# Four interleaved attention layers on one core: a new written order for stages and visits, layer 2's queries projected beside its keys, exps of projections from an SBUF copy

## The chip, the cores and the metric

The kernel runs on 1 core of a Trainium2 chip. The metric is the device time of one execution in microseconds; before the change it is 2619.29 us, the median of 3 runs (2614.57 to 2623.58). Line numbers (L1292) are those of the kernel before.

## The reference

x has 2048 tokens of 1024 features. Four layers follow one another: A, B, A, B, numbered 0 to 3 in the code. Each is `x = x + layer(layernorm(x))`, with 32 heads of 32 features; the two A layers share their weights, and so do the two B layers.

```python
# A: linear attention
pq = einsum("bhsd,hdf->bhsf", q, w_phi);  pk = einsum("bhsd,hdf->bhsf", k, w_phi)
phi_q = concat([softmax(pq), softmax(-pq)], -1);  phi_k = concat([softmax(pk), softmax(-pk)], -1)
kv = einsum("bhsf,bhsd->bhfd", phi_k, v);  z = einsum("bhsf->bhf", phi_k)
o = einsum("bhqf,bhfd->bhqd", phi_q, kv) / (einsum("bhqf,bhf->bhq", phi_q, z)[..., None] + 1e-6)
return o @ wo
# B: full softmax attention, no mask
p = softmax(einsum("bhqd,bhkd->bhqk", q, k) * 32**-0.5);  o = einsum("bhqk,bhkd->bhqd", p, v)
return o @ wo
```

In an A layer, kv and z need the keys and values of all 2048 tokens before the first output. In a B layer every query needs every key, but sums over keys can be collected in parts.

## The kernel before, in words

The 2048 tokens are 16 tiles of 128 (t or tg) and 4 chunks of 512 (c). The 1024 features are 8 groups of 128 (g, four heads each). A projection is a *task*: eight matmuls that sum over the features into one PSUM bank of 128 x 512 (`mm8`), and a `post` that empties the bank.

**The stages.** `AK` projects keys (with w_phi folded into the weights by `fold`) and values of an A layer, takes two exps of each key bank (of x and of -x, L737, on ACT), normalises them and sums kv and z in `kvacc`. `PQ` projects its queries for one chunk, with two exps of each bank (L841). `DN` forms the denominators and the outputs, `AO` the output projection, residual and layernorm. `BP` projects keys (into K2a, K2b), queries (to DRAM as qd) and values (V) of a B layer for one chunk and one half of the features. `BO` is its output projection. `PQ` needs the same transposed, normalised input (xnT) as `AK` of its chunk, so `spill` writes that input to DRAM (xs, 1 MB a chunk, POOL's queue) and `xslot` loads it again. xnT has two slots, and a third in kvacc while kvacc is not in use; they are granted in the order of the list `users`.

**Attention of a B layer** runs in *units*: a query range of 4 or 2 tiles, a pair of heads and some chunks of keys. A visit in the tuple `VISITS` is (first tile, tiles, chunks of keys, adds a stored part, finishes, half of the groups), and it stands for 8 units. Part sums that aren't finished go to DRAM (pd) and come back. A step of a unit is a few matmuls for scores into two double-bank tiles of PSUM (ring, three of them; L1312), an exp of 128 x 1024 on ACT for each (L1292, tile E), and matmuls of E with V and with ones into the bank acc (L1348). There are 2048 such exps, 1024 in each B layer; the model calls them exp_chain.

**Who sets the order.** Every engine's instruction order is written out when the kernel is built. A small clock in the kernel (`Clock`) imitates the engines with costs (MM, SEM, c_ps, c_act and others) and decides what is issued next. An attention step goes first whenever its unit is ready and two ring tiles are free; otherwise `pick` looks through the next 60 undone tasks, in the order in which the stages were built, and takes the first whose inputs, weight slab, buffers and bank are there. Within a unit list the visits are strictly in order. While attention is active (`att_active`), a background task has the single bank bg and its matmuls are split in four column strips (L402); when it isn't, free ring tiles serve as more banks, and matmuls are whole (L405). Then too, evictions (`cp`, L381 and L383) may go to ACT as well as DVE. While attention is active, the two exps of a key or query bank first wait 0.5 us of the clock's time (ACT_SLACK), and release the bank after the second.

Weights are slabs of 1 MB. Four slots hold them always; the stores of V and K2 serve as more when no attention uses them. POOL's queue loads them. SP's queue issues the other transfers and the DMA transposes of normalised inputs and A outputs. For chunks in the set `TR`, PE transposes those instead (`pe_tr`, L462), with an eviction. SBUF temporaries are 28 blocks of 128 x 1024 (`blk`); tokens such as t_phi, t_eq (8 each) limit how many blocks one kind may hold.

Of the kernel before, what the change touches and what calls it, by code (L numbers as in the profile page):

```python
# [18 lines left out]
P = 128  # L19
# [10 lines left out]
MM = 0.216  # L30
SWITCH = 0.105
SEM = 0.1
# [78 lines left out]
class Clock:  # L111
# [50 lines left out]
    def _op(self, gen, eng, cost, fn, lat=SEM):  # L162
        if isinstance(eng, tuple):
            eng = min(eng, key=lambda e: max(self.busy.get(e, 0.0), self.now))
# [51 lines left out]
class Task:  # L216
# [17 lines left out]
VISITS = (  # L234
# [29 lines left out]
def kernel(  # L264
# [72 lines left out]
    t_q, t_acc, t_part, t_R, t_tmp, t_ot = tok(2), tok(5), tok(6), tok(2), tok(3), tok(8)  # L337
# [11 lines left out]
    xsp = {(l, c): dd(f"xs{l}_{c}", [P, PO, C]) for l in (0, 2) for c in range(NC)}  # L349
# [58 lines left out]
    users = [(0, "K", c) for c in range(NC)]  # L408
    for l in (0, 2):
        if l == 2:  # L410
            users += [(2, "K", 0), (2, "K", 1), (2, "K", 2), (2, "Q", 0), (2, "K", 3)]
        else:
            users += [(0, "Q", 0)]
        users += [(l, "Q", 1), (l + 1, "B", 0), (l + 1, "B", 1), (l, "Q", 2), (l + 1, "B", 2),
                  (l, "Q", 3), (l + 1, "B", 3)]
# [29 lines left out]
    def ln_tail(u, t, xb, st):  # L445
# [6 lines left out]
        yield ("op", "V", c_sb(1024, 4), lambda e: nc.vector.tensor_scalar(  # L452
# [119 lines left out]
    def slab_plan():  # L572
        want = sorted((slab_next(s), s) for s in slab_use)
        for nxt, s in want[:12]:
# [8 lines left out]
            for i, sl in enumerate(slots):  # L583
                if not sl.avail or sl.users or sl.loading:
                    continue
                if i >= 4 and min((x for x in sl.limits if x > lo[0]), default=1 << 30) < nxt:
                    continue
# [119 lines left out]


    phi_b = {}
# [7 lines left out]
    def build_AK(l, c, prs=(0, 1), hs=(0, 1)):  # L717
        u = (l, "K", c)
        if u in TR and 0 in hs:
            for pr in prs:  # L720
# [3 lines left out]
        if 0 in prs and 0 in hs:  # L724
            clk.start(xslot(u, 17))
            clk.start(spill(u))

        def pk(t, h):
            tg = 4 * c + t

            def post(bank, rel, b):
                use_xn(u)
                e = b
                if att_active():
                    yield ("sleep", ACT_SLACK)
                for s in range(2):
                    yield ("op", "S", c_act(C), lambda x, s=s: nc.scalar.activation(  # L737
                        out=e[:, s * C:(s + 1) * C], in_=bank[:], func=ACT.Exp, scale=1.0 - 2.0 * s))
                rel()
# [5 lines left out]
                yield tt(("V", "P") if att_active() else "V", {"V": c_sb(1024), "P": c_pool(1024)}, e3, e3, rb, ALU.mult)  # L745
# [18 lines left out]
        def kv(pr, h, gi):  # L764
            tgs = [4 * c + 2 * pr, 4 * c + 2 * pr + 1]
# [3 lines left out]
            def mms():  # L769
                o = []  # L770
                for j, idx in enumerate(GRP[gi]):
                    gl, s = divmod(idx, 2)
                    for a, tg in enumerate(tgs):
                        def fn(bank, ct, W, j=j, gl=gl, s=s, a=a, tg=tg):
# [5 lines left out]
                                start=(j == 0 and a == 0), stop=(a == 1), skip_group_check=True)  # L780
# [3 lines left out]
            def post(bank, rel, b):  # L784
# [8 lines left out]
                if c == 0 and pr == 0:  # L793
# [4 lines left out]
                kv_n[l] = kv_n.get(l, 0) + 1  # L798
                if c == NC - 1 and pr == 1:
# [12 lines left out]
            add(f"kv{l}.{c}.{pr}.{h}.{gi}", needs, None, mms(), post)  # L812

        for h in hs:
# [4 lines left out]
            for pr in prs:  # L819
                for gi in range(3):  # L820
                    kv(pr, h, gi)
# [6 lines left out]
    n_cnt = {}  # L828

    def build_PQ(l, c):  # L830
# [3 lines left out]
        def pq(g):  # L834
            def post(bank, rel, b):
                use_xn(u)
                e = b
                if att_active():
                    yield ("sleep", ACT_SLACK)
                for s in range(2):  # L840
                    yield ("op", "S", c_act(C), lambda x, s=s: nc.scalar.activation(  # L841
                        out=e[:, s * C:(s + 1) * C], in_=bank[:], func=ACT.Exp, scale=1.0 - 2.0 * s))
                rel()
# [130 lines left out]
    def build_BP(l, c, h):  # L974
        u = (l, "B", c)
        if h == 0:
            clk.start(xslot(u, 24))
# [5 lines left out]
        def kk(g):  # L983
            gl = g % 4

            def post(bank, rel, b):
                use_xn(u)
                b4 = bank[:].rearrange("p (m e n) -> p m e n", m=2, e=2)
                yield cp(K2[0][c][h][:, gl], b4[:, :, 0, :], 256)
# [6 lines left out]
                None, ks_no[h, c // 2])  # L996

        def qq(g):
            gl = g % 4

            def post(bank, rel, b):
# [4 lines left out]
                for x in (0, 64):  # L1006
                    yield ("op", "V", c_sb(C, 4), lambda e, x=x: nc.vector.tensor_copy(
# [7 lines left out]
        def vv(t, h):  # L1015
            def post(bank, rel, b):
                use_xn(u)
                yield cp(Vc[c][h][:, t, :], bank[:], C)
                rel()
                clk.set(("V", l, c, t, h))  # L1020
            add(f"bv{l}.{c}.{t}.{h}", [("xt", u, t)], ("bv", h),
                mm8(lambda k, W: xn[u][:, k, t * P:(t + 1) * P], lambda k, W: W(k)), post,
                None, vs_no[h, c // 2])

        kk(4 * h)
        qq(4 * h)
        for t in range(4):
            vv(t, h)
# [470 lines left out]
```

## Time and profile before

| what | before |
|---|---|
| median of 3 runs | 2619.29 us |
| profiled execution, its own time | 2628.97 us |
| its span, first to last instruction | 2626.8 us |
| TensorE (PE) busy | 2304.8 us, 88% |
| ScalarE (ACT) busy | 2105.4 us, 80% |
| VectorE (DVE) busy | 1262.1 us, 48% |
| GpSimd (POOL) busy | 426.3 us, 16% |
| attention exps on ACT (L1292) | 2048, 1908.5 us |
| mean granted TensorE clock | 0.906 of full |
| first and last attention exp | 301.4 and 2612.8 us |

All times inside the execution are microseconds from the span's start. Busy time counts instructions in progress, each stretch once; overlapping exps have a mean of 1109 ns but pass every 0.93 us at best. A row of a group of instructions gives line, engine, operation, output<-inputs, shape and count, then busy time and mean ns of one, then idle time of the engine just before them and what ended it. A row of a stretch gives its bounds and length, busy times with counts, then the granted clock and DMA figures.

### The profile page before, as it was taken

What the parts mean: (1) busy time and instruction counts of PE and PEld (TensorE: products, weight loads), DVE (VectorE), ACT (ScalarE), POOL (GpSimd) and SP (SyncE); (2) the same over time, 40 slices, a digit from 0 to 9 for tenths busy, and PEclk for the clock granted to TensorE, in tenths of its full rate; (3) what the DMA queues carried; (4) which work ended last, traced back from release to release, by engine and by line L of the source; (5) the groups of instructions that cost most, each with busy time, mean ns of one, the idle gap of its engine ahead of it and who ended that gap; (6) DMA issues with size and microseconds to landing.
All of it is one profiled execution on the core that took longest, in us unless ns stands there. A gap on an engine that the chain in (4) does not pass through costs nothing. (4 is left out here: it accounts for less than half of the span.)

```text
span 2626.8 us, 65988 instructions
## 1 busy us (share of the span) xinstructions
PE 2304.8 (88%) x28190; PEld 925.2 (35%) x28250; DVE 1262.1 (48%) x2246; ACT 2105.4 (80%) x2443; POOL 426.3 (16%) x519
## 2 busy tenths in 40 slices
PE   6887898898999998998888889889899989899887
PEld 3444432333333222343444443233333322223333
DVE  5874741432344555874447575143244354464222
ACT  3533379597999999999993337959798999999998
POOL 3131200100110222331122220010021021122010
PEclk9998999899999989999999899989989998778777
DMA  7382562464353333342023345246334322231000
GB/s 241 109 212 85 163 203 97 131 164 141 78 147 116 122 98 124 90 140 55 26 80 113 117 134 169 93 127 180 111 106 147 113 90 77 81 100 49 18 20 21
DMA packets 198998, 294.79 MB, mean 112 GB/s; under 512 B 89904, under 2 KB 100144, under 8 KB 195632
## 3 DMA queue, kind: packets, MB, share of 16 engines
q1 hardware_dynamic: 171072, 176.28, 23.2%
q0 software_dynamic: 27632, 114.31, 13.2%
q8 instruction: 220, 3.60, 0.6%
q14 instruction: 74, 0.61, 0.1%
HBM read 191.95 MB, written 79.69 MB: 103 GB/s over the span
## 5 line engine op out<-in xcount | busy, mean ns | idle before, releaser
L1292 ACT ACTIVATE E<-ring 128x1024 bf16<-128x1024 f32 x2048 | 1908.5, 1109 | 152.8 <-PE ring L1312 150.7
L1348 PE MATMUL acc<-E,V 128*32 128x512 bf16 (+1 forms) x5120 | 710.7, 380 | 4.0 <-DVE blk L388 2.2
L1348 PE MATMUL acc<-E,ones 128*32 128x512 bf16 (+1 forms) x5120 | 710.4, 380 | 0.0
L1312 PE MATMUL ring<-Q,K2b 32*128 32x512 bf16 (+1 forms) x2560 | 438.7, 369 | 161.8 <-ACT E L1292 154.3
L1312 PE MATMUL ring<-Q,K2a 32*128 32x512 bf16 (+1 forms) x2560 | 459.6, 370 | 10.9 <-ACT E L1292 10.1
L1348 PEld LDWEIGHTS <-V 128*32 128x32 bf16 x5120 | 206.3, 101 | 309.9 <-issue 278.8
L1087 DVE COPY blk<-acc 128x512 f32<-128x512 f32 (+1 forms) x160 | 93.3, 583 | 428.3 <-PE acc L1348 419.9
L388 POOL TENSOR_TENSOR blk<-blk,blk 64x512 bf16<-64x512 f32 (+1 forms) x156 | 168.7, 1081 | 714.1 <-DVE blk L1121 643.2
L1312 PEld LDWEIGHTS <-K2a 32*128 32x128 bf16 x2560 | 123.6, 93 | 427.9 <-issue 420.7
L1312 PEld LDWEIGHTS <-K2b 32*128 32x128 bf16 x2560 | 155.0, 93 | 289.7 <-issue 284.3
L1121 DVE RECIPROCAL blk<-blk 128x128 f32<-128x128 f32 x252 | 223.0, 923 | 2.3
L388 DVE TENSOR_TENSOR blk<-blk,acc 128x512 f32<-128x512 f32 x128 | 87.3, 682 | 275.3 <-PE acc L1348 274.6
L1348 PEld LDWEIGHTS <-ones 128*32 128x32 bf16 x5120 | 201.6, 101 | 2.4 <-issue 0.4
L402 PE MATMUL bg<-slab,blk 128*32 128x512 bf16 x2532 | 170.8, 386 | 3.2 <-DVE blk L388 2.0
L402 PE MATMUL bg<-slab,xnT 128*32 128x512 bf16 x2076 | 152.2, 414 | 11.0 <-ACT blk L737 9.1
L402 PE MATMUL bg<-xnT,slab 128*32 128x512 bf16 x1596 | 113.0, 399 | 9.6 <-ACT blk L841 4.8
L405 PE MATMUL ring<-slab,xnT 128*128 128x512 bf16 x426 | 105.0, 386 | 12.9 <-DMA xnT<-blk 3.2
L388 DVE TENSOR_TENSOR blk<-blk,bg 128x512 bf16<-128x512 bf16 x106 | 72.1, 680 | 85.0 <-PE bg L402 76.7
L388 POOL TENSOR_TENSOR blk<-blk 128x256 bf16<-128x256 f32 x102 | 73.5, 730 | 227.3 <-DVE blk L388 226.3
L405 PEld LDWEIGHTS <-xnT 128*128 128x128 bf16 x729 | 71.4, 100 | 101.2 <-issue 18.4
L402 PEld LDWEIGHTS <-blk 128*32 128x32 bf16 x2896 | 78.2, 98 | 73.7 <-issue 16.2
L742 DVE TENSOR_REDUCE sm<-blk 128x32 f32<-128x1024 bf16 x64 | 77.5, 1212 | 50.3 <-ACT blk L737 50.1
(187 smaller groups left out, 2337.5 us busy)
## 6 DMA issues: line engine op xcount, KB each, us to landing
pd<-blk SPq DMA_DIRECT2D x128, 256.0 KB, 2.3
blk<-pd SPq DMA_DIRECT2D x128, 256.0 KB, 3.1
slab<-in_B_wqkv_dram POOLq DMA_DIRECT2D x28, 1024.0 KB, 7.3
Q<-qd SPq DMA_DIRECT2D x112, 256.0 KB, 2.7
qd<-blk SPq DMA_DIRECT2D x64, 256.0 KB, 2.2
x<-blk SPq DMA_DIRECT2D x48, 256.0 KB, 2.2
blk<-x SPq DMA_DIRECT2D x48, 256.0 KB, 4.0
slab<-in_A_wo_dram POOLq DMA_DIRECT2D x10, 1024.0 KB, 6.2
```

What stands on the lines that cost most here:

```text
L388: return ("op", e, cost, lambda x: eng(x).tensor_tensor(out=o, in0=a, in1=b, op=op))
L402: nc.tensor.matmul(o[js], lhsT=l[:, js], rhs=r, start=st, stop=sp, tile_position=(0, 32 * j), skip_group_check=True)
L405: nc.tensor.matmul(o, lhsT=l, rhs=r, start=st, stop=sp, skip_group_check=True)
L742: yield ("op", "V", c_sb(1024), lambda x: nc.vector.reduce_sum(out=sm[:, 0:32], in_=e3, axis=AX.X))
L1087: yield ("op", "V", c_ps(n), lambda e: nc.vector.tensor_copy(out=a, in_=acc_t[:, 0:n]))
L1121: yield ("op", "V", 0.1 + 0.0065 * P, lambda e, x=x: nc.vector.reciprocal(out=r[:, x:x + P], in_=r[:, x:x + P]))
L1292: yield ("op", "S", c_act(2 * n), lambda x: nc.scalar.activation(out=E[:, :, 0:n], in_=ring_t[buf][:, :, 0:n], func=ACT.Exp, scale=INV_SQR ...
L1312: nc.tensor.matmul(ring_t[bufs[e]][:, j, i * n:(i + 1) * n], lhsT=K2[e][c][u.g // 4][r, u.g % 4, m, :], rhs=u.Q[r, e, 0:n], start=True, st ...
L1348: nc.tensor.matmul(u.acc[r0 + 32 * j:r0 + 32 * j + 32, 0:n], lhsT=lh, rhs=E[:, j, i * n:(i + 1) * n], start=first, stop=final, tile_positi ...
```

## The change

It replaces the written-out list of stages by a table `STAGES` and the visits by two tables, `VIS1` and `VIS3`, one for each B layer. A visit now names single groups (0 to 7, four heads each) instead of a half; layer 1 has 24 visits (64 group loads of queries, 128 units), layer 3 has 29 (80 and 160); before, each had 18 (72 and 144). `BP` is cut into quarters of the features, and a unit waits for its quarter of V alone.

Layer 2's queries: `PQ(2, c)` goes. `PS(2, c)` projects them from the xnT of `AK(2, c)`, stores each bank as bf16 in DRAM (pqd, 128 KB, SP's queue), and `pq_loader` brings them back once layer 2's last keys have their input, for the two exps from SBUF. The spill and reload of layer 2's xnT goes.

`two_exps`: while attention is active, DVE copies a key or query bank to an SBUF block and releases the bank; both exps read the block. Otherwise they read the bank as before.

Beside that: kv sums of four tiles at once where a stage has both pairs (`KVM`; 81 tasks for 96 over a pair of layers as the table cuts them); normalising of phi_k may go to POOL also without attention; first weight loads spaced by 8 us; other chunks transposed by PE (`TR`); 26 blocks for 28; costs of the clock changed, among them MM2, SEM, PE_LAT and a choice of engine by end of work.

```diff
-VISITS = (
-    (0, 4, (0,), False, False, 0), (0, 4, (0,), False, False, 1),
-    (4, 4, (0, 1), False, False, 0), (0, 4, (1,), True, False, 0),
...
+VIS1 = (
+    (0, 4, (0,), False, False, (0, 1)), (0, 4, (1,), True, False, (0, 1)), (0, 4, (0, 1), False, False, (2, 3)),
+    (4, 4, (0, 1), False, False, (0, 1, 2, 3, 4, 5, 6, 7)), (0, 4, (0, 1), False, False, (6, 7)),
+    (0, 4, (0, 1), False, False, (4, 5)), (8, 4, (0, 1, 2), False, False, (4, 5)),
+    (8, 4, (0, 1, 2), False, False, (6, 7)), (0, 4, (2, 3), True, True, (0, 1, 2)),
...
+    (14, 2, (0, 1, 2, 3), False, True, (0, 3, 6, 7)), (14, 2, (0, 1, 2, 3), False, True, (4, 5)),
+    (14, 2, (0, 1, 2, 3), False, True, (1, 2)),
+VIS3 = (
+    (0, 4, (0,), False, False, (0, 1, 2, 3, 4, 5)), (0, 4, (0,), False, False, (6, 7)),
+    (0, 4, (1,), True, False, (0, 1)), (0, 4, (1,), True, False, (2, 3)),
...
+STAGES = (
+    ('AK', 0, 1, (0, 1), (0,)), ('AK', 0, 0, (0,), (0,)), ('fold', ('pk', 1)), ('AK', 0, 2, (1,), (0,)),
...
+    ('PQ', 0, 1), ('PQ', 0, 0), ('DN', 0, 2), ('PQ', 0, 2), ('BP', 1, 0, (0, 1, 2)), ('BP', 1, 1, (0, 1)),
+    ('BP', 1, 2, (0, 1)), ('BP', 1, 1, (2, 3)), ('BP', 1, 0, (3,)), ('PQ', 0, 3), ('AO', 0, 2), ('DN', 0, 3),
...
+    ('PS', 2, 0), ('BO', 1, 11, 13), ('BO', 1, 4, 8), ('BO', 1, 10, 11), ('AK', 2, 1, (1,), (1,)),
+    ('BO', 1, 0, 1), ('PS', 2, 1), ('AK', 2, 0, (0, 1), (1,)), ('AK', 2, 2, (0,), (0,)), ('BO', 1, 13, 15),
+    ('AK', 2, 2, (1,), (0,)), ('PS', 2, 2), ('BO', 1, 15, 16), ('AK', 2, 1, (0, 1), (0,)),
...
+    ('AK', 2, 3, (1,), (1,)), ('DN', 2, 0), ('PS', 2, 3), ('BP', 3, 0, (0, 1)), ('AO', 2, 1),
...
-users = [(0, "K", c) for c in range(NC)]
...
+    users = []
+    for sg in STAGES:
+        if sg[0] in ("AK", "PQ", "BP") and (sg[0], sg[1]) != ("PQ", 2):
...
+    def two_exps(e, bank, rel):
+        src, tmp = bank[:], None
+        if att_active():
+            tmp = yield from grab(t_cp)
+            src = tmp[:].bitcast(F32)
+            yield ("op", "V", c_ps(C), lambda x: nc.vector.tensor_copy(out=src, in_=bank[:]))
+            rel()
+        for s in range(2):
+            yield ("op", "S", c_act(C), lambda x, s=s: nc.scalar.activation(
+                out=e[:, s * C:(s + 1) * C], in_=src, func=ACT.Exp, scale=1.0 - 2.0 * s))
+        if tmp is None:
+            rel()
+        else:
+            drop(t_cp, tmp)
...
-                if att_active():
-                    yield ("sleep", ACT_SLACK)
-                for s in range(2):
-                    yield ("op", "S", c_act(C), lambda x, s=s: nc.scalar.activation(
-                        out=e[:, s * C:(s + 1) * C], in_=bank[:], func=ACT.Exp, scale=1.0 - 2.0 * s))
-                rel()
+                yield from two_exps(e, bank, rel)
...
-                yield tt(("V", "P") if att_active() else "V", {"V": c_sb(1024), "P": c_pool(1024)}, e3, e3, rb, ALU.mult)
+                yield tt(("V", "P"), {"V": c_sb(1024), "P": 2.0}, e3, e3, rb, ALU.mult)
...
+    def build_PS(l, c):
+        u = (l, "K", c)
+        def pq(g):
+            def post(bank, rel, b):
+                use_xn(u)
+                yield cp(b[:, 0:C], bank[:], C)
+                rel()
+                yield dma(pqd[c, g][:], b[:, 0:C], 128)
+                drop(t_q, b)
+                clk.set(("pqd", c, g))
+            gl = g % 4
+            add(f"ps{l}.{c}.{g}", [("xnT", u)], ("pq", g // 4),
+                mm8(lambda k, W: W(k)[:, gl * P:(gl + 1) * P], lambda k, W: xn[u][:, k, :]), post, t_q)
+        for g in range(G):
+            pq(g)
+    def pq_loader():
+        yield ("key", ("xnT", (2, "K", 3)))
+        for c in range(NC):
+            for g in range(G):
+                yield ("key", ("pqd", c, g))
+                e = yield from grab(t_eq)
+                clk.start(pq_load1(c, g, e))
+    def pq_load1(c, g, e):
+        yield dma(e[:, 0:C], pqd[c, g][:], 128)
+        if att_active():
+            yield ("sleep", ACT_SLACK)
+        for s in (1, 0):
+            yield ("op", "S", c_act(C), lambda x, s=s: nc.scalar.activation(
+                out=e[:, s * C:(s + 1) * C], in_=e[:, 0:C], func=ACT.Exp, scale=1.0 - 2.0 * s))
+        eq_b[2, c, g] = e
+        clk.set(("eq", 2, c, g))
...
-NBLK = 28
+NBLK = 26
+KVM = True
+T_BULK = 8.0
 ACT_SLACK = 0.5
-TR = {(0, "K", 0), (2, "K", 3), (0, "O", 0), (2, "O", 0), (1, "B", 0), (3, "B", 0)}
+TR = {(0, 'K', 0), (0, 'K', 1), (2, 'K', 1), (2, 'O', 0), (2, 'O', 3)}
```

More of the change, by code (lines that the diff above doesn't have):

```diff
@@ L718, in build_AK @@
         u = (l, "K", c)
-        if u in TR and 0 in hs:
-            for pr in prs:
+        new = not xslot_on.get(u)
+        if u in TR:
+            for pr in [x for x in prs if (u, x) not in xslot_on]:
+                xslot_on[u, pr] = True
                 for t in (2 * pr, 2 * pr + 1):
@@ L837, in post @@
                 e = b
[L838 to L843, printed above, removed]
+                yield from two_exps(e, bank, rel)
                 eq_b[l, c, g] = e
```

212 lines of the change are left out of this document (99 added, 113 removed), and 36 rows, old and new, of tables (STAGES, VIS1, VIS3, VISITS).

## The prediction

> **What bounds the kernel now.** I read the page's totals first, then cut the span into stages where the attention exps start and stop, then looked at what the background projections wait for inside a stage.
>
> ```profile
> span 2626.8 us, 65988 instructions
> PE 2304.8 (88%) x28190; PEld 925.2 (35%) x28250; DVE 1262.1 (48%) x2246; ACT 2105.4 (80%) x2443; POOL 426.3 (16%) x519
> ...
> L1292 ACT ACTIVATE E<-ring 128x1024 bf16<-128x1024 f32 x2048 | 1908.5, 1109 | 152.8 <-PE ring L1312 150.7
> ...
> 0.00:301.00 301.00, 238.97 (x1631) 130.31 (x1656) 206.43 (x394) 108.38 (x191) 74.36 (x117) 0.95 0.53 154
> 301.00:650.00 349.00, 307.63 (x3575) 115.40 (x3583) 125.37 (x248) 269.61 (x312) 31.95 (x46) 0.94 0.51 157
> 650.00:1050.00 400.00, 369.52 (x4682) 126.07 (x4675) 195.50 (x334) 391.80 (x432) 66.82 (x67) 0.92 0.39 113
> 1050.00:1389.00 339.00, 293.09 (x5310) 133.99 (x5313) 197.90 (x317) 325.25 (x369) 77.49 (x85) 0.94 0.26 76
> 1389.00:1552.00 163.00, 139.40 (x953) 75.56 (x963) 107.67 (x208) 46.20 (x81) 40.37 (x58) 0.93 0.35 118
> 1552.00:1900.00 348.00, 306.83 (x3513) 113.63 (x3519) 127.58 (x253) 264.47 (x304) 27.30 (x39) 0.93 0.46 141
> 2614.00:2627.00 13.00, 7.79 (x39) 3.09 (x32) 5.35 (x7) 0.00 (x0) 0.00 (x0) 0.89 0.10 40
> ```
>
> After the stretch and its length the columns are PE, PEld, DVE, ACT and POOL busy, the granted clock, the DMA share and GB/s. Of the 2048 attention exps (1908.5 us of ACT, 0.93 us each at full pace) none runs in the head (0 to 301), almost none in the middle (1389 to 1552) and none in the tail (13 us). These three make 477 us. The same stretches for the exps alone:
>
> ```profile
> 301.00:650.00 349.00, 253.55 (x270) 0.94 0.51 157
> 650.00:1050.00 400.00, 389.41 (x423) 0.92 0.39 113
> 1050.00:1389.00 339.00, 315.77 (x334) 0.94 0.26 76
> 1552.00:1900.00 348.00, 249.75 (x265) 0.93 0.46 141
> 1900.00:2150.00 250.00, 238.64 (x260) 0.95 0.39 114
> 2150.00:2614.00 464.00, 461.01 (x501) 0.77 0.17 54
> ```
>
> Length less exps gives what attention loses: 95 and 98 us in the two ramps (301 to 650, 1552 to 1900), 11 and 23 in the rest of layer 1, 11 and 3 in the rest of layer 3, together 242. So 1908.5 + 477 + 242 = 2627, the span. Exps can't shrink; everything that the change can win lies in the 719 us. In the ramps attention has used up the chunks of keys that are projected and ACT waits, while PE still idles 41 us in each (349 - 307.6, 348 - 306.8). Why PE idles there, the timeline shows:
>
> ```profile
> 420.50 0.98 PE L402 MATMUL bg<-xnT,K2a 128*32 128x512 bf16 x8 [0.69 <-ACT blk L841]
> ...
> 424.48 0.60 PE L402 MATMUL bg<-xnT,K2b 128*32 128x512 bf16 x8
> ...
> 427.33 0.60 ACT L841 ACTIVATE blk<-bg 128x512 bf16<-128x512 f32 x1
> ...
> 429.62 0.64 ACT L841 ACTIVATE blk<-bg 128x512 bf16<-128x512 f32 x1
> ...
> 430.31 0.61 PE L402 MATMUL bg<-xnT,K2a 128*32 128x512 bf16 x8 [0.69 <-ACT blk L841]
> ...
> 450.00:500.00 50.00, 40.45 (x444) 14.57 (x445) 12.69 (x26) 39.26 (x46) 2.00 (x3) 0.79 0.40 133
> ...
> 850.00:900.00 50.00, 23.03 (x352) 1.00 0.38 125
> ```
>
> While attention runs, background work has one PSUM bank. A query group ends its matmuls near 425.1, but its two exps queue behind attention's on ACT and free the bank only at 430.3: 9.8 us from group to group. The last row is L402 alone (the background's column-split matmuls): 352 are 11 groups of 32, so 4.55 us a group where DVE empties the bank. An exp-held bank costs 5.3 us more.
>
> **The change, part by part.** How many groups do this is counted from the exps, first L841 (queries), then L737 (keys), two a group:
>
> ```profile
> 301.00:650.00 349.00, 19.94 (x32) 0.94 0.51 157
> 1389.00:1552.00 163.00, 17.47 (x32) 0.93 0.35 118
> 1552.00:1900.00 348.00, 19.89 (x32) 0.93 0.46 141
> ...
> 650.00:1050.00 400.00, 6.31 (x9) 0.92 0.39 113
> 1050.00:1389.00 339.00, 24.39 (x35) 0.94 0.26 76
> ...
> 1414.43 1.89 PE L405 MATMUL bg<-xnT,V 128*128 128x512 bf16 x8
> 1416.16 1.89 PE L405 MATMUL ring<-slab,xnT 128*128 128x512 bf16 x7
> ```
>
> A group's own PE time is 1.73 us (1416.16 - 1414.43).
>
> *Ramp of layer 3.* Its 16 query groups leave (chunks 2 and 3 of layer 2's queries): 16 x 1.73 = 28 us of PE and 16 x 9.8 = 157 us of the bank. Their exps stay on ACT, now from reloaded copies that hold no bank. If PE's work alone sets the ramp, 28 is won; at most PE's idle 41 goes too, 69; if the new visits (29 for 18) only shift the shortage, it may lose 10. I take 45, near the middle of 28 and 69, because work and bank both leave.
>
> *Ramp of layer 1.* Its 16 query groups stay, but DVE's copy (0.69 us, last fence of this part) frees the bank: 16 x 5.3 = 84 us of bank time. PE idles 41 there, the ceiling; the floor is in the slower rival below. I take 20, half the ceiling, as nothing but waiting leaves.
>
> *Rest of layer 1 (650 to 1389).* Chunks 0 to 2 of layer 2's queries come in, 24 groups: 41.5 us of PE into 76 idle (739 - 369.5 - 293.1), and 24 x 4.55 = 109 us of bank time. The 22 key groups (44 exps) release 22 x 5.3 = 116. The bank comes out even and PE has room, so I take 0: +41 if PE's idle time is all forced, -20 if the copies win more of the 34 us that attention loses there.
>
> *Middle.* 16 query groups leave (chunks 0 and 1, 28 us), 8 come (chunk 3, 14 us): -14. Transposes of layer 2's last keys and of layer 3's first chunk go from PE to DMA, and the whole chain to the next exp hangs on them:
>
> ```profile
> 1396.88 1.89 PE L405 MATMUL ring<-V,blk 128*128 128x512 bf16 x8
> ...
> 1408.82 1.89 PE L405 MATMUL ring<-V,blk 128*128 128x512 bf16 x8
> ...
> 1412.28 0.72 PE L462 MATMUL ring<-ident,blk 128*128 128x128 bf16 x10
> 1413.04 1.01 ACT L381 COPY xnT<-ring 128x1024 bf16<-128x1024 bf16 x1 [16.77 <-PE ring L462]
> ...
> xnT<-blk SPq DMA_TRANSPOSE x40, 4.0
> ...
> 11.31 1.04 PE L462 MATMUL bg<-ident,blk 128*128 128x128 bf16 x8 [11.31 <-DVE blk L452]
> 29.69 3.60 PE L405 MATMUL bg<-slab,xnT 128*128 128x512 bf16 x8 [5.33 <-DMA xnT<-blk]
> ...
> L383 DVE CAST blk<-bg 128x512 bf16<-128x512 f32 x54 | 37.2, 689 | 95.5 <-PE bg L402 91.6 <-PE bg L405 3.9
> ```
>
> 1.8 us by PE (1412.28 to 1414.05), 4.0 by DMA: +2.2 at each of two places, +4. Output projections of token tiles 12 to 15 run here in one piece, eight groups from 1396.88 to 1410; tiles 12 and 13 now have an earlier place: 4 groups, up to -7, taken as -4. The middle: -14. Bounds: -35 (the 16.8 us ACT gap filled as well) to +10 (the new DMAs late: DN of chunk 0 waits for eight reloads and 16 exps, which the 16 groups of the last keys cover; without that cover 16 x 0.6 = 10).
>
> *Head.* Chunk 1's transposes go from DMA to PE, which ends the 5.3 us wait at 29.69; two others (first attention output, first chunk of layer 1) go the other way, +4. Later weight loads may bring the first matmul forward from 11.3. I take -4, between -20 and +25.
>
> *Taken at nothing.* Copies for 38 groups and evictions for 32 add 70 x 0.69 = 48 us to DVE, which is 48% busy; if no cover held, 48 is their price. The kv sums merged (96 to 81 a pair of layers) and normalising shared with POOL take DVE work away. 64 more transfers on SP's queue, each behind SP's transposes and reloads, replace 8 of 1 MB on POOL's. Units go from 144 to 128 (layer 1) and 160 (layer 3), each with one 0.69 eviction.
>
> The sum: -45 - 20 + 0 - 14 - 4 = -83; 2627 - 83 = 2544, and 2.2 lie around the span (2628.97 for the profiled execution). That execution is 9.7 above the median of 2619.29, so (2544 + 2.2) x 2619.29 / 2628.97 = 2537.
>
> Exps from SBUF occur nowhere in this trace. [...]
>
> **Rivals.** *The bank was the whole shortage.* For it: the 9.8 us turnaround, and the clock of 0.79 with PE at 40.45 of 50 exactly while exps held the bank (450 to 500). Against: PE is 88% busy over both ramps. Both ramps then reach their ceilings and the rest its better bounds: -69 - 41 - 20 - 25 - 10 = -165, which gives 2455. [...]
>
> *Work moved, not removed.* PE's 2305 us stay as they are. If layer 1 pays for its 24 groups (+41) and only layer 3's 28, the middle's 14 and the head's 4 are won, the span falls by 5: 2614, no change. For it: PE 90% busy in 650 to 1389. Against: its 76 idle. In this case it would also be true that copies don't do what they are there for.
>
> *Chunks wanted sooner.* The new visits of layer 1 want chunk 1 after 16 exps, before after 64, and chunk 3 after 352, before after 448. That takes 48 + 96 exps = 134 us of cover from the projections. Chunk 3's 40 groups (8 queries, 8 outputs, 24 of layer 1) at 4.55 need 182 us; 192 exps (178 us) stood ahead of chunk 3 with chunk 2 there, now 96 (89). In full this is +134: 2627 - 83 + 134 = 2678, 2670 at the median; it decides from about 90 us on. Against: where ACT waits, groups run back to back at 1.73 instead of 4.55, so later chunks arrive early if the head is stretched, and the query chunks done early feed the output projections that are missing later.
>
> **How the numbers follow.** Forecast 0.53, bank 0.22, moved work 0.12, sooner 0.13. The likeliest gives 2537, its own range 2490 to 2590. For 8 in 10 the range takes in the bank case down to 2455 and moved work with a part of the price of the third: 2455 to 2630. About 0.3% (8 us) is what a measurement can tell from no change here. Faster: 0.53 + 0.22 + 0.05 of moved work + 0.02 = 0.82; same 0.06; slower 0.12.
>
> **What would show it.** L841 gone from the ramp of layer 3 as a bank holder, and that ramp's loss near 53 us instead of 98; groups behind query and key exps at about 4.6 us; the ramp of layer 1 near 75; 650 to 1389 with as much loss as before; middle near 149. Ramp 1 plus head longer than 396 would mean that the visits cost their cover; an unchanged ramp 3 would mean that PE's work and not the bank set it. A time over 2630, or a gain that comes mostly out of the head, would make the prediction wrong.

## The result and the profile after

The changed kernel takes 2467.46 us, the median of 4 runs (2465.78 to 2470.49). The kernel before takes 2620.03 beside it. The ratio is 0.9421, with a 95% interval of 0.9401 to 0.944. The gain of 153 us is nearly twice the 82 that I forecast; the time comes near that of the rival that called the bank the whole shortage (2455).

The page of the changed kernel, its totals and its group of attention exps (L1361 is what L1292 was):

```profile
span 2464.0 us, 68772 instructions
PE 2236.2 (91%) x29569; PEld 920.3 (37%) x29569; DVE 1276.4 (52%) x2289; ACT 2121.1 (86%) x2488; POOL 388.7 (16%) x465
...
L1361 ACT ACTIVATE E<-ring 128x1024 bf16<-128x1024 f32 x2048 | 1905.3, 1183 | 24.8 <-PE ring L1381 24.4
```

The exps are the same 2048 and cost the same 1905 us. Most of what was won is idle time of ACT ahead of them, nearly all of it behind PE's scores: 24.8 us, where it was 152.8. PE has more instructions and is still 69 us less busy. The last section comes back to that.

The stretches of the changed kernel follow, cut where its attention starts and stops (first exp at 336, end of layer 1 at 1340, layer 3 from 1479 to 2452). The columns are those of the rows before: PE, PEld, DVE, ACT, POOL, granted clock, DMA share, GB/s.

```profile
0.00:336.00 336.00, 282.55 (x1979) 151.76 (x1979) 221.30 (x441) 133.21 (x242) 84.61 (x126) 0.98 0.53 161
336.00:670.00 334.00, 315.35 (x4537) 124.49 (x4533) 134.53 (x270) 313.28 (x356) 22.29 (x30) 0.99 0.43 131
...
1340.00:1479.00 139.00, 119.32 (x808) 60.48 (x805) 98.29 (x209) 55.81 (x101) 24.85 (x33) 0.99 0.51 145
1479.00:1800.00 321.00, 300.25 (x4256) 114.52 (x4259) 136.42 (x272) 310.24 (x348) 23.96 (x32) 0.97 0.52 159
...
2100.00:2452.00 352.00, 316.59 (x4689) 120.19 (x4687) 136.25 (x218) 346.47 (x376) 55.20 (x56) 0.76 0.15 48
```

The same view for the attention exps alone:

```profile
336.00:670.00 334.00, 304.36 (x328) 0.99 0.43 131
670.00:1000.00 330.00, 326.65 (x354) 0.94 0.32 102
1000.00:1340.00 340.00, 328.84 (x345) 0.99 0.32 101
...
1479.00:1800.00 321.00, 301.75 (x327) 0.97 0.52 159
1800.00:2100.00 300.00, 297.19 (x324) 0.89 0.45 139
2100.00:2452.00 352.00, 346.47 (x376) 0.76 0.15 48
```

Length less exps is what attention loses. The ramps lose 30 (334 - 304.4) and 19 us, where they lost 95 and 98. The rest of layer 1 loses 14 instead of 34, the rest of layer 3 loses 8 instead of 14. The granted clock in the ramps is 0.99 and 0.97, where it was 0.94 and 0.93.

The whole change by stages, from the first and last attention exp of each layer:

| stage | before | after | measured | forecast |
|---|---|---|---|---|
| head | 301.4 | 336.1 | +35 | -4 |
| layer 1 | 1087.9 | 1002.9 | -85 | -20 |
| middle | 162.6 | 140.3 | -22 | -14 |
| layer 3 | 1061.9 | 972.1 | -90 | -45 |
| tail | 13.0 | 12.5 | 0 | 0 |
| span | 2626.8 | 2464.0 | -163 | -83 |

The stages are those of the two profiled executions. The one of before took 2628.97 us, 9 above its median, so the table shows 163 us where the medians show 153.

The turnaround of the bank, in the timeline of the changed kernel's first ramp (columns: start, duration, engine, line, what; in brackets what the engine waited for):

```profile
477.14 0.69 DVE L755 COPY blk<-bg 128x512 f32<-128x512 f32 x1 [2.30 <-PE bg L446]
...
478.77 1.90 PE L446 MATMUL bg<-xnT,slab 128*32 128x512 bf16 x32
480.77 0.69 DVE L755 COPY blk<-bg 128x512 f32<-128x512 f32 x1 [2.94 <-PE bg L446]
...
481.34 0.89 ACT L758 ACTIVATE blk<-blk 128x512 bf16<-128x512 f32 x1
481.62 1.68 PE L446 MATMUL bg<-xnT,slab 128*32 128x512 bf16 x28
483.67 0.90 ACT L758 ACTIVATE blk<-blk 128x512 bf16<-128x512 f32 x1
```

DVE starts its copy as the 32 matmuls end, and PE starts the next group 0.16 us after the copy (480.77 + 0.69 to 481.62). The two exps run while that group is under way. Group to group it is 2.85 us here (481.62 - 478.77), where it was 9.8; I had expected about 4.6.

### The profile page after: what moved, and what is told of

Its sections match the earlier page's. It is cut to its first block, busy times and chain, and to the rows that moved or that the text cites. A ratio compares the mean times of both kernels' runs of the same rounds, so it can differ in the third digit from the quotient of the medians.

```text
span 2464.0 us, 68772 instructions
## 1 busy us (share of the span) xinstructions
PE 2236.2 (91%) x29569; PEld 920.3 (37%) x29569; DVE 1276.4 (52%) x2289; ACT 2121.1 (86%) x2488; POOL 388.7 (16%) x465
## 4 chain that ended last, share of the span: by engine, by line
PE 46%; ACT 20%; issue 6%; DVE 4%; DMA 1%; ACTq 0%; POOL 0%; DVEq 0%; POOLq 0%
ACT E L1361 18%; PE bg L446 14%; PE acc L1417 14%; PE ring L1381 13%; PE ring L449 3%; DVE blk L432 1%; PE bg L449 1%; DMA xnT<-blk 1%; ACT blk L758 1%; DVE blk L1230 0%; ACT blk L919 0%; DVE blk L1223 0%; DVE sm L799 0%; DMA kvacc<-blk 0%; PE ring L988 0%
## 5 line engine op out<-in xcount | busy, mean ns | idle before, releaser
L1361 ACT ACTIVATE E<-ring 128x1024 bf16<-128x1024 f32 x2048 | 1905.3, 1183 | 24.8 <-PE ring L1381 24.4
L1417 PE MATMUL acc<-E,V 128*32 128x512 bf16 (+1 forms) x5120 | 694.6, 372 | 2.8 <-ACT E L1361 2.1
L1417 PE MATMUL acc<-E,ones 128*32 128x512 bf16 (+1 forms) x5120 | 694.4, 372 | 0.0
L1381 PE MATMUL ring<-Q,K2b 32*128 32x512 bf16 (+1 forms) x2560 | 433.0, 364 | 118.2 <-ACT E L1361 110.6
L1381 PE MATMUL ring<-Q,K2a 32*128 32x512 bf16 (+1 forms) x2560 | 451.7, 366 | 8.5 <-ACT E L1361 8.2
L1417 PEld LDWEIGHTS <-V 128*32 128x32 bf16 x5120 | 199.9, 99 | 298.5 <-issue 271.8
L446 PE MATMUL bg<-xnT,slab 128*32 128x512 bf16 x2912 | 192.7, 382 | 5.8 <-DVE K2b L427 2.1
L446 PE MATMUL bg<-slab,blk 128*32 128x512 bf16 x2560 | 171.6, 386 | 0.5
L446 PE MATMUL bg<-slab,xnT 128*32 128x512 bf16 (+1 forms) x2496 | 150.2, 361 | 1.6 <-DVE blk L755 0.6
L446 PEld LDWEIGHTS <-slab 128*32 128x32 bf16 x3688 | 101.2, 97 | 104.3 <-issue 21.3
L758 ACT ACTIVATE blk<-ring 128x512 bf16<-128x512 f32 x84 | 47.3, 597 | 97.1 <-PE ring L449 75.9
L427 DVE CAST blk<-bg 128x512 bf16<-128x512 f32 x74 | 51.0, 690 | 123.6 <-PE bg L446 115.9
L446 PEld LDWEIGHTS <-blk 128*32 128x32 bf16 x2904 | 80.2, 98 | 68.9 <-issue 11.8
```

The costliest lines, as they stand in the source:

```text
L427: eng(e).tensor_copy(out=o, in_=i)
L446: nc.tensor.matmul(o[js], lhsT=l[:, js], rhs=r, start=st, stop=sp, tile_position=(0, 32 * j), skip_group_check=True)
L1361: yield ("op", "S", c_act(2 * n), lambda x: nc.scalar.activation(out=E[:, :, 0:n], in_=ring_t[buf][:, :, 0:n], func=ACT.Exp, scale=INV_SQR ...
L1381: nc.tensor.matmul(ring_t[bufs[e]][:, j, i * n:(i + 1) * n], lhsT=K2[e][c][u.g // 4][r, u.g % 4, m, :], rhs=u.Q[r, e, 0:n], start=True, st ...
L1417: nc.tensor.matmul(u.acc[r0 + 32 * j:r0 + 32 * j + 32, 0:n], lhsT=lh, rhs=E[:, j, i * n:(i + 1) * n], start=first, stop=final, tile_positi ...
```

## The experiments

Each run stands beside the kernel before on the same chip (whose median there was 2619.7 to 2621.1). This table has the stages of all, cut like those above; the text below takes them in turn.

| run | what it is | median | ratio (95%) | head | layer 1 | middle | layer 3 |
|---|---|---|---|---|---|---|---|
| old_copy | before + copies | 2507.61 | 0.9569 (0.9543 to 0.9595) | 306 | 1042 | 130 | 1018 |
| old_copy_held | before + copies, bank kept | 2605.91 | 0.9946 (0.9928 to 0.9965) | 299 | 1077 | 169 | 1052 |
| old_ps | before + queries beside keys | 2557.06 | 0.9756 (0.9728 to 0.9784) | 305 | 1073 | 193 | 975 |
| old_both | before + both | 2490.03 | 0.9501 (0.9478 to 0.9525) | 296 | 1040 | 172 | 966 |
| new_old_order | after, old stages and visits | 2496.34 | 0.9528 (0.9503 to 0.9552) | 288 | 1054 | 169 | 970 |
| new_old_visits | after, old visits | 2531.06 | 0.9661 (0.9644 to 0.9677) | 334 | 1005 | 186 | 995 |
| new_old_stages | after, old stages | 2493.14 | 0.9519 (0.9504 to 0.9533) | 287 | 1090 | 136 | 966 |
| new_tokens | after, larger limits | 2474.75 | 0.9447 (0.9431 to 0.9463) | 341 | 1013 | 139 | 966 |
| new_nocopy | new_tokens without copies | 2523.88 | 0.9633 (0.9609 to 0.9657) | 339 | 1031 | 164 | 979 |
| new_nops | new_tokens, queries by PQ | 2519.61 | 0.9627 (0.9604 to 0.9651) | 337 | 1014 | 179 | 975 |
| new_old_clock | after, old costs of the clock | 2488.20 | 0.9507 (0.9488 to 0.9526) | 343 | 1018 | 142 | 971 |
| new_pe_transposes | after, PE transposes two chunks more | 2473.06 | 0.9442 (0.9428 to 0.9456) | 336 | 1005 | 147 | 970 |

### The copies alone: old_copy

The only edit to the kernel before is `two_exps` for keys and queries, with two blocks for the copies.

```diff
-                if att_active():
-                    yield ("sleep", ACT_SLACK)
-                for s in range(2):
-                    yield ("op", "S", ... in_=bank[:], func=ACT.Exp, ...)
-                rel()
+                yield from two_exps(e, bank, rel)
```

> The kernel before, with one thing of the change: while attention is active, DVE copies a key or query bank to an SBUF block and both exps read the block. Order, visits and queries of layer 2 stay. Bank theory (exps that hold the one background bank are most of what the ramps lack): the 38 groups of exps release 200 us of bank time, the two ramps lose about 55 us each instead of 95 and 98, the rest of layer 1 about 12 instead of 23: some 90 us less than before, about 2530. Order theory (the projections come in the wrong order and number, whatever the bank does): less than 20 us, 2600 or more. Work theory (PE is simply full in the ramps): less than 10 us.

It took 2507.61 us, 113 less than before. DVE made 59 copies (16 in each ramp and 27 for keys in the rest of layer 1); the 38 groups of the expectation were layer 1's alone. The attention exps in its stretches, cut like those of before (a ramp of 349 or 348 us, then the rest):

```profile
306.00:655.00 349.00, 284.08 (x304) 0.99 0.55 162
655.00:1055.00 400.00, 395.17 (x426) 0.94 0.39 119
1055.00:1348.00 293.00, 283.33 (x297) 1.00 0.30 88
1477.00:1825.00 348.00, 283.78 (x303) 0.99 0.49 147
```

The ramps lose 65 and 64 instead of 95 and 98, the rest of layer 1 loses 15 instead of 34. The clock in the ramps is 0.99. The middle is 33 us shorter, because layer 1 leaves less work for it: 761 matmuls and 109 us of PE there instead of 953 and 139.

```profile
1348.00:1477.00 129.00, 108.79 (x761) 58.96 (x771) 85.26 (x178) 37.49 (x64) 29.51 (x43) 0.95 0.34 114
```

So the copies alone are worth more than my whole forecast, and in stages that I had not tied to them.

### Is it the bank, or the copy? old_copy_held

The copy is made and the exps read it, but the bank is given back only after the second exp.

```diff
             yield ("op", "V", c_ps(C), lambda x: nc.vector.tensor_copy(out=src, in_=bank[:]))
-            rel()
         for s in range(2):
             yield ("op", "S", c_act(C), ...)
-        if tmp is None:
-            rel()
-        else:
+        rel()
+        if tmp is not None:
             drop(t_cp, tmp)
```

> The kernel before with DVE's copy for the exps of key and query banks, but the bank is released only after both exps, as in the kernel before. This parts two reasons for the 113 us that the copies won in the old order. If the release of the bank is the reason, all of it goes: 2615 to 2640, slower than before by DVE's extra work at most. If it is the exps' place in ACT's order, their source in SBUF or the wait of 0.5 us of the clock that went with the old form, most stays: 2510 to 2550.

2605.91 us, 9 below the least that was expected if the release were everything: of the 113, 98 are gone again (2605.91 - 2507.61). The exps of its two ramps, in stretches of old_copy_held:

```profile
298.00:647.00 349.00, 260.75 (x278) 0.95 0.52 158
...
1544.00:1892.00 348.00, 259.07 (x276) 0.94 0.46 142
```

They lose 88 and 89 us, and the clock is back at 0.95 and 0.94. The DVE copies of the first ramp, first with the early release (timeline of old_copy):

```profile
421.43 0.69 DVE L714 COPY blk<-bg 128x512 f32<-128x512 f32 x1 [1.87 <-PE bg L402]
...
425.01 0.69 DVE L714 COPY blk<-bg 128x512 f32<-128x512 f32 x1 [2.89 <-PE bg L402]
...
428.05 0.69 DVE L714 COPY blk<-bg 128x512 f32<-128x512 f32 x1 [1.04 <-PE bg L402]
```

and with the bank kept (timeline of old_copy_held):

```profile
421.43 0.69 DVE L714 COPY blk<-bg 128x512 f32<-128x512 f32 x1 [3.71 <-PE bg L402]
423.62 0.63 ACT L716 ACTIVATE blk<-blk 128x512 bf16<-128x512 f32 x1
...
425.94 0.65 ACT L716 ACTIVATE blk<-blk 128x512 bf16<-128x512 f32 x1
...
429.42 0.69 DVE L714 COPY blk<-bg 128x512 f32<-128x512 f32 x1 [2.74 <-PE bg L402]
```

A group passes every 3.0 to 3.6 us with the release, and every 8.0 us without: the second exp ends at 426.6, 4.5 us after the copy's end at 422.1. Both kernels copy such banks on DVE (59 and 50 of them) and take the exps from the copies; the edits differ in the place of the release alone. The time at which the bank comes free makes the 98 us, together with the order that the kernel's clock writes around it. What makes the 14 that old_copy_held keeps (its exps no longer wait 0.5 us of the clock's time, for one) these runs don't tell.

### The queries alone, and both: old_ps, old_both

`PS(2, c)` follows `AK(2, c)` in the old list of stages, and `PQ(2, c)`, the spill and the reload go. old_both has the copies too.

```diff
+            build_PS(2, 0)
...
+            build_PS(2, 1)
...
+            build_PS(2, 2)
...
-            build_PQ(2, 0)
+            build_PS(2, 3)
...
-        build_PQ(l, 1)
+        if l == 0:
+            build_PQ(l, 1)
...
+    clk.start(pq_loader())
```

> The kernel before, with one thing of the change: layer 2's queries are projected beside its keys, stored and loaded again; exps still hold the bank where they read it. Bank theory: the ramp of layer 3 loses 157 us of bank use and 28 us of PE and comes to about 30 us of loss instead of 98; middle 14 shorter; layer 1 up to 20 longer for its 24 more groups: about 65 less, 2555. Order theory: about 20 less, 2600. Work theory: 28 and 14 won, 41 paid in layer 1: no change, 2620.

> The kernel before with both: copies for the exps and layer 2's queries beside its keys, in the old order. Bank theory: about 130 us less than before, 2490, most of what the whole change gives. Order theory: at most 40 less, 2580. Work theory: 2610 to 2620.

The queries alone: 2557.06 us, 64 less. Layer 3 is 87 us shorter, layer 1 is 15 shorter, but the middle is 30 longer. The exps of its two ramps (stretches of old_ps):

```profile
304.00:653.00 349.00, 255.44 (x272) 0.94 0.51 157
...
1571.00:1919.00 348.00, 324.83 (x352) 0.98 0.47 136
```

The ramp of layer 3 loses 23 where it lost 98, with no copy anywhere. That is 75 us, above the ceiling of 69 that I gave it. The ramp of layer 1, whose 16 query groups still hold their bank through two exps, loses 94 as before.

Both together: 2490.03 us, 131 less than the 2621 beside it, not 113 + 64 = 177. On top of the copies the queries are worth only 18. The stages say why. Layer 3 gains 52 (1018 to 966), and the middle gives 42 back (130 to 172). The middle of old_both:

```profile
1335.00:1507.00 172.00, 147.30 (x977) 77.78 (x988) 118.22 (x232) 59.64 (x102) 36.81 (x52) 0.95 0.42 135
```

PE is busy there for 147.3 us, 38.5 more than in old_copy, which is 22 groups of 1.73. They are not queries: 16 of the 32 query groups are stored in DRAM before 1335 (view of the tile pq) and 16 in the middle, and the middle of old_copy had 16 query groups too. Layer 1 hardly changed (1042 to 1040). In the old order 16 query groups go in, and as much other work or more comes out at its end, into the middle.

### The order: new_old_order, new_old_visits, new_old_stages

The changed kernel with the old list of stages (and the old `TR`), with the old visits (now written by groups; `t_o` 8), or with both.

```diff
-VIS = {1: VIS1, 3: VIS3}
+VISITS = ((0, 4, (0,), False, False, (0, 1, 2, 3)), ...
+VIS = {1: VISITS, 3: VISITS}
-STAGES = (
-    ('AK', 0, 1, (0, 1), (0,)), ('AK', 0, 0, (0,), (0,)), ('fold', ('pk', 1)), ...
+STAGES = (('fold', ('pk', 0)),
+    ('AK', 0, 0, (0, 1), (0,)),
...
-TR = {(0, 'K', 0), (0, 'K', 1), (2, 'K', 1), (2, 'O', 0), (2, 'O', 3)}
+TR = {(0, "K", 0), (2, "K", 3), (0, "O", 0), (2, "O", 0), (1, "B", 0), (3, "B", 0)}
```

> The changed kernel with the old order: stages, visits and the chunks that PE transposes as before, queries of layer 2 placed right behind each chunk's keys, all else as changed (quarters of V, merged kv sums, clock costs, spaced loads). Bank theory: 2480 to 2500, near the changed kernel's 2467. Order theory: 2560 to 2600. Against the same kernel without the small edits (old kernel with both) the small edits are worth under 15 us by either.

> The changed kernel with the visits of before in both B layers (18, halves of the groups), stages as changed, with 8 blocks of A outputs in flight for 4. It parts the order's share (new order 2467, old order 2496) between visits and stages. If chunks wanted sooner cost their cover, the old visits win back part of the 40 us by which the head grew, and the time is 2450 to 2465. If the finer visits are what the order wins (output projections can start sooner), it is 2480 to 2500.

> The changed kernel with the new visits but the stages of before, and the chunks that PE transposes as before. If the stages carry the order's share, 2490 to 2510, as with both old; if the visits do, 2465 to 2480; if the two were found together and fit only each other, slower than either pair, above 2510.

With both old: 2496 us, within 7 of old_both. The small edits (kv sums, POOL's share, weights spaced, costs of the clock) together are worth nothing in the old order. So the new order is worth 29 us (2496 to 2467). One half of it alone brings 3, which the intervals don't tell from nothing (new visits, 2493); the other alone costs 35 (new stages, 2531, with the 8 for `t_o`), outside both ranges that were expected for it.

The head is 287 to 306 in every kernel with the old stages and 334 to 343 in every kernel with the new ones, whatever the visits. The longer head belongs to the stages. What it buys, the attention exps of new_old_stages show (old stages, new visits):

```profile
287.00:637.00 350.00, 247.10 (x258) 0.96 0.53 150
637.00:1037.00 400.00, 389.86 (x420) 0.94 0.38 113
```

and those of new_old_visits (new stages, old visits):

```profile
334.00:683.00 349.00, 305.21 (x331) 0.99 0.48 149
...
1873.00:2520.00 647.00, 619.86 (x673) 0.81 0.22 70
```

New visits on the old stages lose 103 us in the ramp, with copies and all, and layer 1 is 35 us longer than with the old visits (1090 against 1054). That they want chunks 1 and 3 sooner than these come is the likely reason; no run parts it from the visits' finer groups. New stages alone lose 44, and the two together 30. Head and layer 1 in sum are 1339 in the changed kernel and with the new stages alone, 1342 with the old order and 1377 with the new visits alone. With the old visits the longer head takes from layer 1 what it costs itself; a gain it is only with the new visits.

What the visits bring is the middle. The middle of new_old_stages:

```profile
1377.00:1513.00 136.00, 109.13 (x803) 57.92 (x814) 92.43 (x198) 55.96 (x97) 31.81 (x42) 0.99 0.51 160
```

It has 109 us of PE where old_both had 147, and is 136 us long where old_both and new_old_order had 172 and 169. So with the new visits some 22 groups (38.2 / 1.73) more are done beside attention. Eight of them are query groups: 24 of the 32 are stored before the middle, as in the changed kernel, where old_both and new_old_order have 16 (view of the tile pq). That the visits do it by finishing token tiles earlier, so that output projections and layer 2's keys can start earlier, is the likely way, but no run isolates it. New stages with old visits are no cure: their middle is 186, and they lose 27 us late in layer 3.

### The parts taken out of the changed kernel: new_tokens, new_nocopy, new_nops

Parts taken out of the changed kernel need other limits on the blocks, so a control has those limits and nothing else.

```diff
-    t_x, t_xn, t_phi, t_eq, t_o, t_oT = tok(4), tok(3), tok(8), tok(8), tok(4), tok(4)
+    t_x, t_xn, t_phi, t_eq, t_o, t_oT = tok(4), tok(9), tok(8), tok(8), tok(8), tok(4)
-WINDOW = 60
+WINDOW = 90
```

new_nocopy has these and the exps on the bank again (`in_=bank[:]`, `rel()` after them), with the wait of 0.5 us of the clock's time ahead of them. new_nops has them and layer 2's queries by `PQ`:

```diff
-    ('AK', 2, 3, (1,), (1,)), ('DN', 2, 0), ('PS', 2, 3), ('BP', 3, 0, (0, 1)), ('AO', 2, 1),
+    ('AK', 2, 3, (1,), (1,)), ('PQ', 2, 0), ('DN', 2, 0), ('PQ', 2, 2), ('BP', 3, 0, (0, 1)), ('AO', 2, 1),
-            clk.start(xslot(u, 17 if l == 0 else 24))
-            if l == 0:
-                clk.start(spill(u))
+            clk.start(xslot(u, 17))
+            clk.start(spill(u))
-    clk.start(pq_loader())
```

> The changed kernel with more room in three limits: 8 blocks of A outputs in flight instead of 4, 9 of normalised inputs instead of 3, the search through 90 undone tasks instead of 60. It is the ground for the next two, which need that room in this order. By every theory these limits bind nowhere: 2455 to 2480.

> The changed kernel with that room, without copies: the exps of key and query banks read the bank and hold it, as before the change. Bank theory: 33 groups hold the bank 5.3 us longer each, 175 us of bank time, and half to all of what the copies won in the old order comes back: 2520 to 2580. Order theory (the new order hides what holds the bank): under 2490.

> The changed kernel with that room, without the projection of layer 2's queries beside its keys: they come from the spilled and reloaded input in layer 3, each chunk's just ahead of its denominators, as before, with copies for their exps. Work theory as the old order showed it with copies in place (2508 to 2490, 18 us): 2485 to 2500. Bank theory with full price as in the old order without copies (64 us): 2530.

The control took 2474.75. Without the copies it is 49 us more, without `PS` 45 more. In the new order copies are worth less than in the old (113). One likely reason is that there are fewer banks to save: the counts of copies in the changed kernel are 8, 5 and 20 in its three stretches of layer 1 and none in layer 3, together 33; the kernel before had 32 + 22 such banks. DVE's busy time was 1262 before and is 1276, and taking the copies out makes nothing faster: the price that I named for them (48 us if nothing hides them) isn't paid.

The time without `PS` lies between the two that were expected. The middle of new_nops is 179 instead of 139:

```profile
1351.00:1530.00 179.00, 157.30 (x978) 78.97 (x991) 104.85 (x219) 55.09 (x101) 29.15 (x44) 0.97 0.43 120
```

PE is busy there for 157.3 us, in the middle of the changed kernel for 119.3: 38 more, some 22 groups. Of these 16 are query groups: 48 of the 64 exps of that kind in this middle belong to queries, which is 24 groups (chunks 0 to 2), in place of chunk 3's 8. In the new order `PS` shortens the middle by 40 and layer 3 by only 9; in the old order it was layer 3 (87) and a longer middle. What a part is worth depends on where the order puts the work that it frees.

### Two prices: new_old_clock, new_pe_transposes

```diff
-SEM = 0.14
-PE_LAT = 0.27
+SEM = 0.1
+PE_LAT = 0.12
...
-            eng = min(eng, key=lambda e: max(self.busy.get(e, 0.0), self.now) + (cost[e] ...))
+            eng = min(eng, key=lambda e: max(self.busy.get(e, 0.0), self.now))
```

(with the old costs of four DVE instructions), and, in the other kernel:

```diff
-TR = {(0, 'K', 0), (0, 'K', 1), (2, 'K', 1), (2, 'O', 0), (2, 'O', 3)}
+TR = {(0, 'K', 0), (0, 'K', 1), (2, 'K', 1), (2, 'K', 3), (2, 'O', 0), (2, 'O', 3), (3, 'B', 0)}
```

> The changed kernel with the old costs in the clock that writes the order (SEM 0.1, 0.12 us from the last matmul to its reader, the old VectorE costs, the choice of an engine without its work). What is computed and where it may run is the same, only when the clock believes things ready. If the order wins because the clock now believes the right times, most of its 29 us goes: 2485 to 2500. If it wins by the tables alone, 2462 to 2475.

> The changed kernel with layer 2's last keys and layer 3's first chunk transposed by PE again, as before the change. The prediction charged the move to DMA with 2.2 us at each place: 4 us less, 2461 to 2466. If the wait lies under other work now (PE waits 1.6 us for the first such transpose in the changed kernel's middle), no difference: 2465 to 2470; the eight groups of transposes and evictions that PE, ACT and DVE get instead can make it slower, to 2475.

The old costs make the changed kernel 21 us slower, with the same stages and visits: 7 in the head and 15 in layer 1. So most of the order's 29 us is there only with costs that go with it; in the old order (new_old_order against old_both) the same costs won nothing. Transposes by PE at the two places where I charged 4 us for DMA give 2473.06, no gain over 2467.46, and a middle of 147 against 140. The DMA transposes stand in the middle of the changed kernel as a wait of PE of 1.62 us (timeline):

```profile
1362.41 1.47 PE L449 MATMUL ring<-slab,xnT 128*128 128x512 bf16 x6 [1.62 <-DMA xnT<-blk]
```

No version that was run is faster than the changed kernel.

## Why the prediction was right or wrong

**Right: what bounds the kernel.** The 242 us that attention lost, and the bank held by exps as their cause, were the place to look. Of these 242, 171 were won (30 + 14 + 19 + 8 = 71 are left). old_copy and old_copy_held show the cause: the same copies on DVE, only the release moved, 98 us.

**Wrong: the ceiling of layer 3's ramp.** This is the step that failed: of some 80 us that the sum lacks in the table of stages, 45 are layer 3's, 26 those of head and layer 1 together and 8 the middle's. I took as ceiling PE's idle time plus the PE work that leaves (69), and of it 45. Measured: 79 (98 to 19), and 75 with the queries alone (old_ps). "Ceiling" held PE's busy time as a fixed amount of work; but it was busy at a granted clock of 0.93. Counted at full clock, the 306.8 us are 285 (306.8 x 0.93), so by this estimate 63 could be won before any work leaves and some 89 with the 16 groups gone (28 x 0.93 = 26). The 79 and the 75 lie inside it, and the clock there is 0.97 now, 0.98 in old_ps.

**Wrong: half of the ceiling, and the groups that stay, in layer 1's ramp.** "Half, as nothing but waiting leaves" gave 20 of 41. The copies alone won 30 there and 34 in layer 3's ramp, whose groups they served too (old_copy). The changed kernel wins 65 (95 to 30), but there the 16 query groups did not all stay, as I had it. The exps of L841 in the head of the kernel before, and those of L758 (keys and queries) in the head and the first ramp of the changed kernel:

```profile
0.00:301.00 301.00, 17.91 (x32) 0.95 0.53 154
...
0.00:336.00 336.00, 62.21 (x112) 0.98 0.53 161
336.00:670.00 334.00, 12.39 (x16) 0.99 0.43 131
```

The head has 112 now, 64 of keys and 48 of queries, where it had 32 of queries; the ramp has 16 where it had 32. So 8 query groups moved ahead of the first exp, with other work: PE is busy in the head for 283 us instead of 239. Head and ramp belong together: forecast -24, measured +35 - 65 = -30. That this sum nearly fits is in part luck, for neither term does. The 16 groups x 5.3 us of bank (84) did not come back in full either: in old_copy the ramp won 30; the copies won as well in the rest of layer 1 (20), the middle (33) and layer 3 (44).

**Wrong: "the bank comes out even" in the rest of layer 1.** I set 24 groups that come in against 22 banks that come free sooner, at 4.55 us a group. In the ramps a group whose bank DVE empties passes every 2.9 to 3.6 us (timelines above). The rest of layer 1 loses 20 us less instead of the same (34 to 14). Its column-split matmuls, before (L402) and after (L446):

```profile
650.00:1389.00 739.00, 256.87 (x3640) 103.42 (x3636) 0.93 0.33 96
...
670.00:1340.00 670.00, 259.23 (x4040) 109.82 (x4032) 0.96 0.32 101
```

That is 114 groups of 32 in 739 us and 126 in 670: 12 more, not 24, so part of the 24 took the place of other work. In the old order the 16 that came in cost the middle 42 us (old_both against old_copy), a term that the sum did not have. That was the "work moved, not removed" rival at another place than I looked for it. In the changed kernel the visits make room for it.

**Wrong: the head.** I took -4 from the transposes and weights; it is +35. I had read the list of stages for what it removes and not for what it does ahead of the first exp (the 8 query groups and the 44 us of PE above). The test that I named (ramp 1 plus head longer than 396) gives 336 + 30 = 366, so the visits did not cost their cover. "Chunks wanted sooner" is likely real all the same: the new visits cost layer 1 35 us on the old stages, below the 90 from which it would decide. The new stages pay for it ahead of time.

**Middle, DMA transposes, DVE.** -22 for -14, inside the bounds. The +4 for DMA transposes isn't seen. The copies are hidden, as taken. The copies and `PS` overlap: 113 + 64 alone, 131 together. Of these 46, some 35 are layer 3's (44 + 87 alone, 96 together), where both give the bank back to the same ramp.

**The rivals.** The bank rival took the ceilings of both ramps and no price, and came nearest (2455). That is in part chance: it had the head as a gain where it cost 35 us and layer 3's ramp too low, and its -25 and -10 are not the better bounds that the prediction states for middle and head (-35 and -20; with these it gives 2435). "PE's 2305 us stay as they are" fell as busy time: they are 2236. Counted at full clock they did stay: 2088 and 2089 (last section).

## What to carry to other kernels

Where one buffer limits the work behind a busy engine, ask who empties it and what stands ahead of that instruction in its queue: here 59 copies of 0.69 us on DVE, 48% busy before, gave the bank back ahead of two exps that queue behind attention's on ACT, and won 113 us (old_copy), where copies with the bank kept won 14 (old_copy_held). Don't take TensorE's busy time as a fixed amount of work without its granted clock: here 2304.8 us at 0.906 and 2236.2 us at 0.934 give the same product, 2088 and 2089. A written-out order is one thing: its stages, its visits and the costs of its model were worth 29 us together, while its visits alone brought next to nothing and its stages alone cost 35.

## What the runs showed of the hardware that was not expected

**PE's busy time times its granted clock was nearly constant.** It is 2304.8 x 0.906 = 2088 before and 2236.2 x 0.934 = 2089 after. The clock is that of the view of cores, here for the changed kernel:

```profile
core 0: 2464.0 us, clock 0.934
```

The products of layer 1, the middle and layer 3, each at its own clock, sum to 1841 to 1864 in the kernel before and the four made from it (old_copy, old_copy_held, old_ps, old_both), while the busy time of the three alone runs from 1992 to 2058. Less waiting went with a higher clock (PE idle for 322 us of the span at 0.906, for 228 at 0.934), and PE did nearly the same work in less busy time. The first ramp agrees: 41 us idle at 0.94 before, 19 at 0.99 after. The last third of layer 3 does not: its clock is 0.76 (2100 to 2452, above) with ACT busy for 346 and PE for 317 of 352 us. Why the clock is low there isn't settled.

**An exp from SBUF took 0.04 us more, though its row says 0.2.** The rows of exps that stand between attention's last 0.64 us at the median from the bank (before) and 0.84 from SBUF (after). They scatter (0.59 to 0.87 and 0.63 to 1.00), and are no price: two from a copy in old_copy_held, shown above, have 0.63 and 0.65. From its start to that of the attention exp behind it, the median is 0.48 us before (102 pairs) and 0.52 after (66 pairs), and 0.52 in old_copy_held too. One pair of before (its first row, 427.33, stands in the prediction):

```profile
427.81 1.96 ACT L1292 ACTIVATE E<-ring 128x1024 bf16<-128x1024 f32 x2
```

and one of after:

```profile
1329.01 0.89 ACT L758 ACTIVATE blk<-blk 128x512 bf16<-128x512 f32 x1
1329.53 9.53 ACT L1361 ACTIVATE E<-ring 128x1024 bf16<-128x1024 f32 x10
```

0.48 and 0.52. Some 82 such exps run beside attention (66 behind copies, 16 of layer 2's queries), so the price is 3 us, an estimate (82 x 0.04).
